# GFNet and FNet halves on one core: C compared with T instead of multiplied, both halves of A in one pass

## The chip, the cores and the metric

The kernel runs on one NeuronCore of one Trainium2 chip. The metric is the device time of one launch in microseconds: 405.52 us before, the median of 3 runs (404.53 to 407.14). A NeuronCore has engines that run side by side and meet at semaphores: TensorE (PE, matmuls into PSUM), VectorE (DVE, elementwise), ScalarE (ACT, copies and functions), GpSimd (POOL) and SyncE (SP, which issues most of the loads). 16 DMA engines carry all transfers.

## What is computed: the reference

Two unrelated results stand side by side in the output, 2048 x 512 each.

```python
# A (GFNet): a filter in the 2-D spectrum of A_x (1, 2048, 512)
X = jnp.fft.rfft2(x, axes=(-2, -1)) * (w_r + 1j * w_i)
a = jnp.fft.irfft2(X, s=(S, D), axes=(-2, -1))

# B (FNet): real part of a 2-D DFT of B_x, with matrices that are inputs
p = jnp.einsum("bsd,ed->bse", x, dft_hid_re)
q = jnp.einsum("bsd,ed->bse", x, dft_hid_im)
b = jnp.einsum("ts,bse->bte", dft_seq_re, p) - jnp.einsum("ts,bse->bte", dft_seq_im, q)
y = jnp.concatenate([a, b], axis=-1)
```

The sequence matrices (2048 x 2048, called C here) arrive as inputs that hold `np.cos(-2.0 * np.pi * ns / S)` and the sine, as float32. The kernel can't take for granted that they do, but it can test it.

## The kernel before

**B.** A sequence transform with the exact cosines and sines needs no large product: the 2048 points are cut into 16 blocks of 128, `b_fft` runs a 16-point transform on DVE over these blocks (`fft16`), `b_slot` does eight small products with tables (`sq`), and `t_rows` multiplies by the hidden matrices (`wd`, L287). What the input C has more than the exact table T is put right by a second way: `prepare` loads 64 pieces of C and of T, builds four quarters of T out of one by copies on ACT (L249, L250), subtracts (L253, DVE), and adds up the absolute difference (L255, ACT) in a column of `stat`. `b_work` multiplies the difference with x (L328, PE, 512 matmuls in f32r), `keep` rounds the sums into SBUF, `rows` multiplies them with `wd` (L305) and DVE adds the two ways' results (L308), which then go out (L311, L313) on POOL's queue. At the end a matmul sums `stat`; if the sum is above `SMALL` = 2^-13, a branch (L770) recomputes B in full in `_b_from_c`.

**A.** The hidden axis is split in two halves of 256 columns (even and odd frequencies), which pass one after the other through: `hidden_fwd` (additions on DVE, L411 to L418, and POOL, L422 and L423, then matmuls L432 and the sums L435, L436 on DVE); `fft16` over 16 blocks; eight slots (`slot`: four additions on POOL, L495 to L498, a matmul L512, the complex product with the weights on DVE, L540 to L542, the folding L557 to L559, matmuls L578, and L584 to L587 on DVE that add and subtract their results); `ifft16`; and `hidden_inv` (matmuls L672, then DVE). The first half's result goes through HBM (`scratch`) and is read back mirrored by a gather (L656), where the second half adds it (L685, L686).

**Order.** The Tile framework orders each engine's instructions by a simulated timeline. The code steers it: `PACE` says how far the other work may fall behind each of the 64 products of B, and `issue_after` holds an instruction behind another. Every engine then runs its own list strictly in turn; a load whose buffer isn't free holds up the loads behind it on SP.

Of the kernel before, what the change touches and what calls it, by code (L numbers as in the profile page):

```python
# [16 lines left out]
P = 128  # L17
# [3 lines left out]
PACE = [3.2] * 9 + [6.3] * 55  # L21
T_ROWS = list(range(13, 29, 2))
SLOTS = [3, 5, 6, 7, 9, 10, 11, 12]
SMALL = 2.0**-13
# [35 lines left out]
def _tables():  # L60
# [22 lines left out]

    b = np.arange(128)
# [15 lines left out]
    tt = np.zeros((2, 4, 4, 128, 2, 2, 256), np.float32)  # L100
    place = (128 * np.arange(8).reshape(4, 1, 2) + b[:, None]).reshape(-1)
    for tb in range(4):
        t = (512 * tb + np.arange(2)[:, None] + 2 * np.arange(256)).reshape(-1)
        th = _ang(np.outer(place, t), S)
        for m, v in enumerate((np.cos(th), -np.sin(th))):
            tt[m, tb] = v.reshape(tt.shape[2:])
    dm = np.zeros((2, 128, 2, 128))
    di = np.zeros((2, 128, 2, 128))
    j = np.arange(128)
    for half in range(2):  # L110
        f = _freqs(half)
        th = _ang(np.outer(j, f), D)
        c, s = np.cos(th), -np.sin(th)
        if half == 0:
            s[:, 0] = np.cos(np.pi * (j % 2))
            dm[half, :, 0] = np.concatenate([c[:, :64], s[:, :64]], 1)
            dm[half, :, 1] = np.concatenate([c[:, 64:], s[:, 64:]], 1)
        else:
            s[0] = -np.sin(_ang(f * 128, D))
            dm[half, :, 0], dm[half, :, 1] = c, s  # L120
        th = _ang(np.outer(f, j), D)
        c, s = 2 * np.cos(th), -2 * np.sin(th)
        if half == 0:
            c[0] = 1.0
            s[0] = np.cos(np.pi * (j % 2))
            di[half, :, 0] = np.concatenate([c[:64], s[:64]])
            di[half, :, 1] = np.concatenate([c[64:], s[64:]])
        else:
            s[:, 0] = -2 * np.sin(_ang(f * 128, D))
            di[half, :, 0], di[half, :, 1] = c, s  # L130
# [9 lines left out]
        "inv": inv.reshape(8, 128, 256).astype(np.float32),  # L140
        "dm": dm.astype(np.float32),
        "di": di.reshape(2, 128, 256).astype(np.float32),
        "sq": sq.astype(np.float32),
        "tt": tt.reshape(2, 4, 4, 128, 2, 512),
        "m0": m0,
        "far": far,
        "mirror": (256 * np.arange(4)[None] + 128 + (-j % 128)[:, None]).astype(np.int32),
# [4 lines left out]
def kernel(  # L152
# [20 lines left out]
    TT = nc.vector.tensor_tensor  # L173
    STT = nc.vector.scalar_tensor_tensor
    ADD, SUB, MUL = ALU.add, ALU.subtract, ALU.mult

# [10 lines left out]
    ps_p = first.enter_context(tc.tile_pool(name="ps_p", bufs=4, space=PSUM))  # L187
    ps_y = first.enter_context(tc.tile_pool(name="ps_y", bufs=1, space=PSUM))
    ps_a = first.enter_context(tc.tile_pool(name="ps_a", bufs=3, space=PSUM))


    xh = bp.tile([P, 16, D], F32R, name="xh")
    wd_sb = bp.tile([P, 2, 4, D], F32, name="wd", bufs=1)
# [6 lines left out]
    zv = ap.tile([P, 16, 256], F32, name="zv")  # L200
# [4 lines left out]
    with tc.tile_pool(name="wp", bufs=1, side="right") as wp:  # L205
        zero = wp.tile([P, 512], mybir.dt.bfloat16, name="zero")
        nc.vector.memset(zero, 0.0)
        warm = ps_a.tile([P, 512], F32, name="pa")
        for _ in range(9):
            nc.tensor.matmul(warm, zero[:, :P], zero, start=True, stop=True)  # L210

    def raw_pair():
        return bp.tile([P, 2, 512], F32, name="raw", bufs=4)

    def row():
        return bp.tile([P, 516], F32, name="yb", bufs=3)
# [7 lines left out]
    items = [(tb, m, q) for tb in (2, 3, 0, 1) for m in range(2) for q in range(8)]  # L224

    def load_x(q, sd):
        rx = load(pt.rearrange("p o m c i -> p (o m c) i")[:, 2 * q : 2 * q + 2], xb[:, q::8, :])
        nc.scalar.copy(xh[:, q::8], rx)
        TT(out=sd[:, q], in0=rx[:, 0], in1=rx[:, 1], op=ADD)
        TT(out=sd[:, 8 + q], in0=rx[:, 0], in1=rx[:, 1], op=SUB)  # L230

    def load_wd():
        for m in range(2):
            load(wd_sb[:, m], wd[m])

    wr = []

    def round_wd():

        wr.append(bp.tile([P, 2, 4, D], F32R, name="wd", bufs=1))  # L240
        for m in range(2):
            nc.gpsimd.dma_start(wr[0][:, m], wd[m])

    def prepare(i):

        tb, m, q = items[i]
        t = bp.tile([P, 2, 2, 256], F32, name="tt", bufs=2)
        load(t[:, 0].rearrange("p o i -> p (o i)"), tabs["tt"][m, tb, q // 2, :, q % 2])
        nc.scalar.copy(t[:, 1, 0], t[:, 0, 0])  # L249
        nc.scalar.mul(t[:, 1, 1], t[:, 0, 1], -1.0)  # L250
        raw = load(raw_pair(), cm[m, tb, q // 2 :: 4, :, q % 2, :].rearrange("r p t -> p r t"))
        e = bp.tile([P, 2, 2, 256], F32R, name="ec", bufs=2)
        TT(out=e, in0=raw.rearrange("p j (i o) -> p j o i", o=2), in1=t, op=SUB)  # L253
        junk = bp.tile([P, 1024], mybir.dt.bfloat16, name="junk", bufs=1)
        nc.scalar.activation(junk, e.rearrange("p j o i -> p (j o i)").bitcast(F32),  # L255
                             mybir.ActivationFunctionType.Abs, accum_out=stat[:, i : i + 1])
        return e

    ps = {}

    def keep(tb, m, acc):


# [53 lines left out]
    def b_work():  # L317
        pending = []
        ready = prepare(0)
        for i, (tb, m, q) in enumerate(items):  # L320
# [3 lines left out]
            if i + 1 < len(items):  # L324
                ready = prepare(i + 1)
# [562 lines left out]
```

## Time and profile before

| | |
|---|---|
| median of 3 runs | 405.52 us (404.53 to 407.14) |
| profiled execution, own time | 409.68 us |
| its span | 407.9 us |
| granted TensorE clock, mean | 0.927 |
| PE busy | 319.5 us, 78% |
| DVE busy | 326.2 us, 80% |
| ACT busy | 179.8 us, 44% |
| POOL busy | 120.3 us, 29% |
| moved by DMA | 90.47 MB, 222 GB/s |

The span is the time between the first and the last thing in the trace; the execution's own time is 1.8 us longer. "Busy" counts a stretch once, though instructions of an engine can overlap. A row of a group reads: line, engine, operation, tiles written and read, shape, count, then the sum of the durations in us and the mean in ns, then how long the engine stood still before these and what ended most of that. A row of the timeline reads: start, duration, engine, line. Rows of the chain have start, duration and what ran.

### The profile page before, as it was taken

Reading aid. Unit: us, or ns where it says so; the run is one execution under the profiler, and the core shown is the slowest. Engines: PE = TensorE matmul, PEld = TensorE weight load, DVE = VectorE, ACT = ScalarE, POOL = GpSimd, SP = SyncE. Lnnn points to the kernel's source line nnn. Section 1 sums busy time; section 2 is a strip of 40 time slices with the busy share of each in tenths; the row PEclk is TensorE's granted clock in tenths of the full one; section 3 lists DMA queues with packets and bytes.
Section 4 is the critical chain, followed back from the end, with each engine's and each line's share of the span. In section 5 each row is a group of like instructions: output and inputs, shape, how many; then the busy total and the mean of one; then the engine's idle time right before and its main releaser. Section 6 shows DMA issues by size and latency. Waiting matters only on the chain.

```text
span 407.9 us, 4458 instructions
## 1 busy us (share of the span) xinstructions
PE 319.5 (78%) x1247; PEld 219.5 (54%) x1247; DVE 326.2 (80%) x601; ACT 179.8 (44%) x398; POOL 120.3 (29%) x158
## 2 busy tenths in 40 slices
PE   3079967999999699999999878998887789800900
PEld 1058745787666366566566557786564557600300
DVE  4999746886983999979987584789949999897662
ACT  4628735668553154423754243665536337100200
POOL 0000005362047739100005153433395850200120
PEclk9999998999999899999999987999999899955755
DMA  7995699876264476523769996697799773300194
GB/s 247 388 405 158 212 305 308 288 286 228 80 191 163 137 241 178 172 90 139 231 217 354 366 408 255 182 300 232 260 299 352 242 203 100 111 9 13 29 338 153
DMA packets 44767, 90.47 MB, mean 222 GB/s; under 512 B 4544, under 2 KB 8896, under 8 KB 44224
## 3 DMA queue, kind: packets, MB, share of 16 engines
q1 hardware_dynamic: 41184, 76.49, 56.9%
q0 software_dynamic: 3552, 13.63, 8.9%
q8 instruction: 12, 0.20, 0.2%
q14 instruction: 19, 0.16, 0.1%
HBM read 79.62 MB, written 10.49 MB: 221 GB/s over the span
## 4 chain that ended last, share of the span: by engine, by line
PE 44%; DVE 25%; DMA 17%; issue 7%; SPq 2%; ACT 1%; POOL 1%; POOLq 0%; DVEq 0%; ACTq 0%
PE acc L328 15%; PE py L287 11%; DMA tt<-tab_tt 7%; DVE ec L253 6%; PE pa L372 5%; DMA raw<-in_cm 3%; DMA xraw<-in_xa 3%; PE pa L578 3%; PE pa L432 2%; PE py L305 2%; SPq L221 2%; PE acc L305 2%; DMA wsp_sb<-in_wsp 2%; DVE m L540 1%; DMA ft<-tab_fwd 1%
## 5 line engine op out<-in xcount | busy, mean ns | idle before, releaser
L328 PE MATMUL acc<-ec,xh 128*128 128x512 f32 x512 | 147.3, 431 | 32.7 <-DVE ec L253 29.4
L328 PEld LDWEIGHTS acc<-ec,xh 128*128 128x128 f32 x512 | 96.5, 194 | 72.4 <-DVE ec L253 38.3
L253 DVE TENSOR_TENSOR ec<-raw,tt 128x1024 fp32r<-128x1024 f32 x64 | 81.1, 1268 | 24.2 <-ACT tt L250 16.6
L255 ACT ACTIVATE junk<-ec 128x1024 bf16<-128x1024 f32 x64 | 67.6, 1056 | 53.6 <-DVE ec L253 53.1
L287 PE MATMUL py<-wd,pt 128*128 128x512 f32 x128 | 59.9, 608 | 0.6 <-DVE yo L572 0.6
L422 POOL TENSOR_TENSOR vf<-uv 128x256 f32<-128x256 f32 x16 | 17.2, 1073 | 138.5 <-DVE uv L415 68.8
L249 ACT COPY tt<-tt 128x256 f32<-128x256 f32 x64 | 26.0, 407 | 69.5 <-DMA tt<-tab_tt 69.5
L287 PEld LDWEIGHTS py<-wd,pt 128*128 128x128 f32 x128 | 24.3, 195 | 26.3 <-issue 24.8
L672 PE MATMUL pa<-zv,di 128*128 128x512 f32 x32 | 17.8, 692 | 22.3 <-DMA di<-tab_di 22.3
L305 PE MATMUL py<-wd,ps 128*128 128x512 f32 x96 | 27.8, 431 | 3.0 <-DVE yb L308 1.8
L250 ACT ACTIVATE tt<-tt 128x256 f32<-128x256 f32 x64 | 26.6, 416 | 0.0
L305 PEld LDWEIGHTS py<-wd,ps 128*128 128x128 f32 x96 | 19.0, 203 | 9.3 <-DMA wd<-in_wd 2.3
L578 PEld LDWEIGHTS pa<-it,yo 128*128 128x128 f32 x128 | 17.8, 199 | 10.4 <-issue 6.6
L578 PE MATMUL pa<-it,yo 128*128 128x128 f32 x128 | 18.7, 287 | 5.5 <-DVE yo L571 3.4
L672 PEld LDWEIGHTS pa<-zv,di 128*128 128x128 f32 x32 | 6.8, 221 | 29.9 <-issue 27.2
L495 POOL TENSOR_TENSOR t<-zv 64x256 f32<-64x256 f32 x14 | 12.4, 885 | 25.7 <-ACT pt L376 21.1
L313 POOL DMA_INDIRECT out_b<-yb,far x8 | 11.4, 1426 | 27.5 <-DVE yb L308 7.1
L376 ACT COPY pt<-pa 128x256 f32<-128x256 f32 x28 | 17.1, 656 | 5.4 <-PE pa L372 5.4
L432 PEld LDWEIGHTS pa<-dm,vf 128*128 128x128 f32 x128 | 17.4, 203 | 2.5 <-issue 1.3
L675 ACT COPY p<-pa 128x512 f32<-128x512 f32 x8 | 4.6, 581 | 31.7 <-PE pa L672 31.7
L540 DVE TENSOR_TENSOR m<-pa,w 128x512 f32<-128x512 f32 x28 | 18.1, 679 | 0.4 <-issue 0.3
L432 PE MATMUL pa<-dm,vf 128*128 128x128 f32 x128 | 17.6, 287 | 0.6 <-DVE um L679 0.6
(200 smaller groups left out, 515.7 us busy)
## 6 DMA issues: line engine op xcount, KB each, us to landing
raw<-in_cm SPq DMA_DIRECT2D x64, 512.0 KB, 7.1
tt<-tab_tt SPq DMA_DIRECT2D x64, 256.0 KB, 3.4
xraw<-in_xa SPq DMA_DIRECT2D x16, 512.0 KB, 5.6
pt<-in_xb SPq DMA_DIRECT2D x8, 512.0 KB, 7.2
w<-in_wa SPq DMA_DIRECT2D x16, 256.0 KB, 4.0
out_a<-xo POOLq DMA_DIRECT2D x4, 1024.0 KB, 5.8
yb<-tab_sq SPq DMA_DIRECT2D x8, 258.0 KB, 7.5
wd<-in_wd SPq DMA_DIRECT2D x2, 1024.0 KB
```

What stands on the lines that cost most here:

```text
L249: nc.scalar.copy(t[:, 1, 0], t[:, 0, 0])
L250: nc.scalar.mul(t[:, 1, 1], t[:, 0, 1], -1.0)
L253: TT(out=e, in0=raw.rearrange("p j (i o) -> p j o i", o=2), in1=t, op=SUB)
L255: nc.scalar.activation(junk, e.rearrange("p j o i -> p (j o i)").bitcast(F32), mybir.ActivationFunctionType.Abs, accum_out=stat[:, i : i + 1])
L287: nc.tensor.matmul(bank, pt[:, o, m, dc, sl], wd_sb[:, m, dc], start=dc == 0, stop=dc == 3)
L305: nc.tensor.matmul(py, ps[tb][:, m, dc, o, h * P : h * P + P], wr[0][:, m, dc], start=m == 0 and dc == 0, stop=m == 1 and dc == 3)
L328: mm = nc.tensor.matmul(acc[dc], xh[:, q + 8 * j, dc * P : dc * P + P], e[:, j].rearrange("p o i -> p (o i)"), start=q == 0 and j == 0, st ...
L372: nc.tensor.matmul(pa[:, :n], z[:, r, dc * P : dc * P + P], sq[:, r, :n], start=r == 0, stop=r == 1)
L432: nc.tensor.matmul(og, vf[:, g, a].rearrange("p h j -> p (h j)"), dm[:, g], start=True, stop=True)
L540: TT(out=mi, in0=x, in1=w[:, i].unsqueeze(2).to_broadcast([P, 2, 2, 128]), op=MUL)
L578: nc.tensor.matmul(pi[:, g_, i].rearrange("p r j -> p (r j)"), yo[:, i, g_].rearrange("p r f -> p (r f)"), it[:, i], start=True, stop=True)
L672: nc.tensor.matmul(pu[g].rearrange("p (a b) -> p a b", a=4), di[:, gs], v[:, g], start=True, stop=True)
```

## The change

1. C is only compared. `prepare`, the products L328, `keep`, `rows`, the f32r copies of x and `wd`, and L308 are gone. `compare` loads 16 pieces of T (a quarter of it, 513 columns) and 64 pieces of C, takes the difference to bf16 on DVE, reading T backwards for two of the four column blocks and with a column of signs for two, and adds up the absolute values on ACT as before. `t_rows` sends B's rows out itself. `SMALL` goes from 2^-13 to 2^-27, so the branch to `_b_from_c` is taken for smaller differences.
2. Both halves of A pass at once, 512 columns wide. x of A is loaded once; `scratch` and the gathers are gone.
3. Sums that DVE did are accumulated by TensorE in PSUM: the two parts in `hidden_fwd` (L435, L436), those after the inverse slot matmuls (L584 to L589), the two groups of the inverse hidden stage and the mirror images there (L678 to L683).
4. Instead of pools that open and close, four regions of 32 KB a partition are used in turn. PSUM holds 3 tiles of two banks and 2 of one.
5. Instead of `PACE`, two lists say at which of 50 steps of A a piece of B (`B_AT`) and how many compares (`C_AT`) are issued. Steps 0 to 7 are `hidden_fwd`, 8 to 12 `fft16`, 13 to 39 the slots, 40 to 45 `ifft16`, 46 to 49 `hidden_inv`. Two compares are left over for the end.

```diff
-PACE = [3.2] * 9 + [6.3] * 55
-SMALL = 2.0**-13
+B_AT = [0, 0, 1, 1, 2, 2, 3, 3] + [4, 5, 6, 7, 7, 7] + [8, 8, 9, 9, 10, 11, 12, 13] + [17, 23, 29, 35, 40, 41, 43, 45]
+C_AT = [0] * 4 + [2] * 4 + [2] * 5 + [0] + [0, 1, 1] * 8 + [0, 0] + [2] * 6 + [4] * 4
+SMALL = 2.0**-27
...
+    def compare():
+        for pr in range(8):
+            ts = []
+            for m in range(2):
+                t = bp.tile([P, 2, 513], F32, name="tt", bufs=3)
+                nc.sync.dma_start(t, tabs["tt"][pr, m])
+                ts.append(t)
+            for tb in range(4):
+                for m, t in enumerate(ts):
+                    v = t[:, :, 512:0:-1] if tb % 2 else t[:, :, :512]
+                    raw = bp.tile([P, 2, 512], F32, name="raw", bufs=3)
+                    nc.sync.dma_start(raw, cm[m, tb, pr])
+                    d = bp.tile([P, 2, 512], mybir.dt.bfloat16, name="ec", bufs=2)
+                    with tc.issue_after(last[0].ins):
+                        if tb in (1, 2):
+                            k = int(tb == 1 and m == 1)
+                            nc.vector.scalar_tensor_tensor(d, v, odd[:, k : k + 1], raw, op0=MUL, op1=SUB)
+                        else:
+                            nc.vector.tensor_tensor(out=d, in0=raw, in1=v, op=ADD if tb and m else SUB)
+                    i = (pr * 4 + tb) * 2 + m
+                    flat = d.rearrange("p j i -> p (j i)")
+                    nc.scalar.activation(flat, flat, mybir.ActivationFunctionType.Abs, accum_out=stat[:, i : i + 1])
+                    yield 1.2
...
     def t_rows(o, b):
...
-                TT(out=pt[:, o, 0, :, sl], in0=us, in1=v, op=SUB)
-                TT(out=pt[:, o, 1, :, sl], in0=us, in1=v, op=ADD)
+                yn, yf = row()[:, :D], row()[:, :D]
+                TT(out=yn.rearrange("p (c f) -> p c f", c=4), in0=us, in1=v, op=SUB)
+                nc.gpsimd.dma_start(out_b[256 * b : 256 * b + 256, :].rearrange("(i o) d -> o i d", o=2)[o], yn)
+                TT(out=yf.rearrange("p (c f) -> p c f", c=4), in0=us, in1=v, op=ADD)
+                nc.gpsimd.indirect_dma_start(
+                    out=out_b, out_offset=bass.IndirectOffsetOnAxis(ap=far_rows[:, 4 * o + b : 4 * o + b + 1], axis=0),
+                    in_=yf, in_offset=None)
...
+    def hidden_fwd(sd):
+        v = region("zv")
+        dm = part(v, 20, 2304)
+        nc.sync.dma_start(dm, tabs["dm"])
...
+        for i in range(8):
+            raw = part(v, 4 * (i % 3), 2, 2, 256)
+            load(raw, xa[1, :, i])
+            u = part(v, 12 + 4 * (i % 2), 2, 2, 256)
+            TT(out=u[:, 0], in0=raw[:, 0], in1=raw[:, 1], op=ADD)
+            w = raw[:, 0]
+            TT(out=w, in0=raw[:, 0], in1=raw[:, 1], op=SUB)
+            STT(u[:, 1, 0], w[:, 1], m0[:, 1:2], w[:, 0], op0=MUL, op1=ADD)
+            STT(u[:, 1, 1], w[:, 0], m0[:, 0:1], w[:, 1], op0=MUL, op1=ADD)
+            ui, vo = (x.rearrange("p e g (a h j) -> p (e g a) h j", a=2, h=2) for x in (u, raw))
+            nc.gpsimd.tensor_tensor(out=vo[:, :, 0], in0=ui[:, :, 0], in1=ui[:, :, 1], op=ADD)
+            nc.gpsimd.tensor_tensor(out=vo[:, :, 1], in0=ui[:, :, 0], in1=ui[:, :, 1], op=SUB)
+            pd = ps_a.tile([P, 2, 2, 256], F32, name="pa")
+            for g in range(2):
+                for a in range(2):
+                    asl = slice(a * 128, a * 128 + 128)
+                    mm(pd[:, 0].rearrange("p s f -> p (s f)"), raw[:, 0, g, asl],
+                                     dm0[:, g, a : a + 2].rearrange("p s f -> p (s f)"),
+                                     start=g == 0 and a == 0, stop=g == 1 and a == 1)
...
+            nc.scalar.copy(sd[:, i::8].rearrange("p s (e f) -> p s e f", e=2), pd.rearrange("p e s f -> p s e f"))
...
+    def slot(e, zv, mid):
...
+        pi = ps_a.tile([P, 2, 2, 256], F32, name="pa")
+        for h in range(2):
+            for g in range(2):
+                for i in range(2):
+                    mm(pi[:, h, g], yo[:, i, h, g], it[:, i], start=i == 0, stop=i == 1)
...
+    def hidden_inv(i, zv):
...
+        for h in (1, 0):
+            for kb in range(2):
+                for g in range(2):
+                    mm(pu[h][:, kb].rearrange("p (a b) -> p a b", a=4), di[:, h, g, kb], v[:, h, g],
+                                     start=g == 0, stop=g == 1)
+        um = part(rb[0], 16 + 4 * (i % 2), 2, 512)
+        nc.scalar.copy(um, pu[1])
+        for h, op in enumerate((ADD, SUB)):
+            xo = part(rb[0], 24 + 4 * h, 2, 512)
+            TT(out=xo, in0=pu[0], in1=um, op=op)
+            nc.gpsimd.dma_start(out_a[256 * h : 256 * h + 256, cols].rearrange("(k p) s -> p k s", p=P), xo)
...
+    while b_at or n < 50:
+        next(a, None)
+        while b_at and b_at[0] <= n:
+            b_at.pop(0)
+            with tc.issue_after(mma[0].ins), tc.issue_after(last[0].ins):
+                next(b, None)
+        for _ in range(C_AT[n]):
+            with tc.issue_after(loads[-1].ins) if n < 8 else ExitStack():
+                next(c)
+        n += 1
```

In all, 62 compares stand at steps (8 in steps 4 to 7, 10 in 8 to 12, 16 among the slots, 12 in 40 to 45, 16 in 46 to 49) and the two left over behind them. `B_AT` puts the loads of B's x at steps 0 to 3, its transform at 4 to 7, its slots at 8 to 13, four `t_rows` among A's slots and four in 40 to 45.

More of the change, by code (lines that the diff above doesn't have):

```diff
@@ L109, in _tables @@
-    j = np.arange(128)
[L110 to L130, printed above, removed]
+    th = _ang(np.outer(np.arange(S), np.arange(513)), S)
@@ L203 @@
     nc.vector.memset(ones, 1.0)
[L205 to L213, printed above, removed]
+    zero = bp.tile([P, 2, 512], mybir.dt.bfloat16, name="ec", bufs=2)[:, 0]
+    nc.vector.memset(zero, 0.0)
+    warm = ps_a.tile([P, 2, 512], F32, name="pa")
+    for _ in range(9):
+        nc.tensor.matmul(warm[:, 0], zero[:, :P], zero, start=True, stop=True)
     def row():
-        return bp.tile([P, 516], F32, name="yb", bufs=3)
+        return bp.tile([P, 516], F32, name="yb", bufs=YB)
     loads = []
@@ L232, in load_wd @@
     def load_wd():
+        rb.append(region("big"))
+        wd_sb.append(part(rb[0], 0, 2, 4, D))
         for m in range(2):
[L234 to L257, printed above, removed]
```

630 lines of the change are left out of this document (247 added, 383 removed).

## The prediction, made before the changed kernel was run

> **What bounds the kernel now.** I read the page's first two parts, then the chain, then the groups by cost.
>
> ```profile
> span 407.9 us, 4458 instructions
> PE 319.5 (78%) x1247; PEld 219.5 (54%) x1247; DVE 326.2 (80%) x601; ACT 179.8 (44%) x398; POOL 120.3 (29%) x158
> PE   3079967999999699999999878998887789800900
> DVE  4999746886983999979987584789949999897662
> PEclk9999998999999899999999987999999899955755
> ```
>
> Two engines share the span: PE and DVE are each at work four fifths of it, and neither has a long empty stretch before the last tenth. So taking work from one alone would stop at the other.
>
> ```profile
> PE 44%; DVE 25%; DMA 17%; issue 7%; SPq 2%; ACT 1%; POOL 1%; POOLq 0%; DVEq 0%; ACTq 0%
> L328 PE MATMUL acc<-ec,xh 128*128 128x512 f32 x512 | 147.3, 431 | 32.7 <-DVE ec L253 29.4
> L253 DVE TENSOR_TENSOR ec<-raw,tt 128x1024 fp32r<-128x1024 f32 x64 | 81.1, 1268 | 24.2 <-ACT tt L250 16.6
> L287 PE MATMUL py<-wd,pt 128*128 128x512 f32 x128 | 59.9, 608 | 0.6 <-DVE yo L572 0.6
> L305 PE MATMUL py<-wd,ps 128*128 128x512 f32 x96 | 27.8, 431 | 3.0 <-DVE yb L308 1.8
> L308 DVE TENSOR_TENSOR yb<-py,pt 128x512 f32<-128x512 f32 x12 | 8.2, 682 | 5.1 <-PE py L305 5.1
> L541 DVE TENSOR_TENSOR y<-m,m 128x256 f32<-128x256 f32 x16 | 8.4, 528 | 0.1
> ```
>
> PE heads the chain, and its costliest group, L328, is the product with C minus T that the change drops. With L305, which multiplies that product by B's second matrix, PE loses over half of its busy time. What is left to set the end is DVE, so I count DVE. Its durations overlap in a row of instructions; the step from start to start is what one costs:
>
> ```profile
> 360.37 0.68 DVE L611 TENSOR_TENSOR E<-T 128x512 f32<-128x512 f32 x1
> 360.97 0.68 DVE L612 TENSOR_TENSOR E<-T 128x512 f32<-128x512 f32 x1
> ...
> 362.17 0.41 DVE L613 SCALAR_TENSOR_TENSOR E<-T 128x256 f32<-128x256 f32 x1
> 362.51 0.41 DVE L614 SCALAR_TENSOR_TENSOR E<-T 128x256 f32<-128x256 f32 x1
> ...
> 387.44 1.22 DVE L685 TENSOR_TENSOR xo<-up,um 128x1024 f32<-128x1024 f32 x1
> 388.57 1.22 DVE L686 TENSOR_TENSOR xo<-up,um 128x1024 f32<-128x1024 f32 x1
> ```
>
> 256 elements a partition cost 0.34 us, 512 cost 0.60, 1024 cost 1.13: 0.07 + 1.04 per 1000 elements. By this line 1536 cost 1.67, 2048 cost 2.20, 128 cost 0.20, and a tiny one 0.07.
>
> **DVE, part by part** (before, then after, us, undisturbed steps):
> - Compare: 64 x 1.13 = 72.6 in both. Half now multiplies by a column of signs first, and 32 of 64 read T backwards. No row shows a backward read; L253 itself reads every second element of C, and its middle duration, 1216 ns in the row further down, is that of L686 in a straight run, so I take nothing. Ends: nothing, or a doubling of 32 of them, +36.
> - A's forward hidden stage: 16 x (0.60 + 4 x 0.34) = 31.4; after, 8 x (2 x 0.60 + 2 x 0.34) = 15.0, since the additions at L435 and L436 become accumulated matmuls.
> - A's 16-point transform: per half 2 x 1.13 + 2 x 0.87 + 0.60 + 26 x 0.34 = 13.4, twice 26.8; after, in one pass as B's, 2 x 2.20 + 2 x 1.67 + 1.13 + 26 x 0.60 = 24.5.
> - Slots: per half and e 2 x 0.60 (L540), 3 x 0.34 (L541, L542, L557), 2 x 0.20, 2 x 0.07, and 0.34 + 2 x 0.20 for L584 to L587: 3.5 x 16 = 56, with e = 0's extras 59. After: 2 x 1.13 + 3 x 0.60 + 2 x 0.34 + 2 x 0.07 = 4.9 x 8 = 39, with extras 42.
> - Inverse 16-point: 2 x (34 x 0.34 + 12 x 0.60) = 37.5; after, 34 x 0.60 + 12 x 1.13 = 34.0.
> - Inverse hidden: 4 x 2 x 0.60 + 4 x (2 x 0.60 + 2 x 1.13) = 18.6; after, 8 x 1.13 = 9.0.
> - L308's additions: 16 x 0.60 = 9.6; after, nothing.
> - Unchanged: loading B 9.6, B's transform 24.5, t_rows 9.6, small ones 1.
>
> Sums: 300 before, 242 after, so 58 less. The page has 326 busy, 26 over my 300. The surplus is seen here (the first and third rows give least, middle and greatest ns):
>
> ```profile
> L253 DVE TENSOR_TENSOR ec<-raw,tt x64: 1202/1216/1875, 21.1 to 341.4; 128x1024 fp32r<-128x1024 f32 x64
> ...
> 134.83 0.96 DVE L542 TENSOR_TENSOR y<-m,m 128x256 f32<-128x256 f32 x1
> ...
> L495 POOL TENSOR_TENSOR t<-zv x14: 719/738/1714, 117.2 to 329.2; 64x256 f32<-64x256 f32 x14
> ```
>
> An operation that takes 0.41 alone took 0.96 beside POOL's, and POOL's own range from 0.72 to 1.71: the two hold each other up. Before, POOL ran 88 such additions (L422, L423, L495 to L498), 88 x 0.72 = 63 us undisturbed. After, it runs 44 of double size; no row has that size, so between 0.72 and 1.44 each, 32 to 63 us. With the surplus in proportion (26 for 63) that is 13 to 26; I take the middle, 20. DVE busy after: 242 + 20 = 262.
>
> **PE.** Steps from the chain:
>
> ```profile
> 107.90 2.59 PE pa L372 x12
> 187.75 3.43 PE py L287 x8
> 191.18 3.75 PE acc L328 x16
> 377.22 3.76 PE pa L672 x4
> ```
>
> A record of 512 columns costs 0.43 in f32 (two records to a matmul), 0.23 in f32r, and 256 columns 0.22. After: B's slots 128 x 0.22 = 28; forward hidden 64 matmuls, 128 x 0.22 = 28; t_rows with the extra row 136 x 0.43 = 58; A's slots 28 x 0.43 + 16 x 0.22 + 128 x 0.22 = 44; inverse hidden 32 matmuls, 64 x 0.43 = 28. Sum 186 against 262 for DVE. The sums that move here double the forward hidden, inverse slot and inverse hidden groups, 3 x 14 = 42 us of PE's free time.
>
> **DMA, ACT, queues.**
>
> ```profile
> HBM read 79.62 MB, written 10.49 MB: 221 GB/s over the span
> raw<-in_cm SPq DMA_DIRECT2D x64, 512.0 KB, 7.1
> 5.74 0.69 DVE L229 TENSOR_TENSOR sdb<-pt 128x512 f32<-128x512 f32 x1 [4.44 <-DMA pt<-in_xb]
> ...
> 15.49 0.69 DVE L229 TENSOR_TENSOR sdb<-pt 128x512 f32<-128x512 f32 x1
> ```
>
> Seven loads of 0.524 MB in 9.75 us are 376 GB/s. After: C 33.6 MB, T 8.4 (16 loads instead of 64), x of A 4.2 (once), x of B 4.2, wd 2.1 (once), sq 2.1, w 4.2, it 2.1, the small tables 2.4, outputs 8.4; scratch is gone. 72 MB are 191 us: no bound as a whole, but one in two places. At the head (steps 0 to 3) dm, four x of A and eight x of B, 7.5 MB, take 20 us plus the first 5, so they end near 25, while DVE has 4 x 1.9 + 9.6 = 17 us to do. At the end (steps 46 to 49 and the rest) 18 compares with T and A's output are 9.4 + 2.1 + 4.2 = 15.7 MB or 42 us, where DVE has 18 x 1.13 + 9.0 = 29 us. Some loads run ahead in three buffers; I add 7 us.
>
> ACT loses L249 and L250, and with them the wait of L253 for L250 (16.6 us above); what is late next for a compare is its load. POOL's queue takes the 16 stores of B's rows, moved from the end into the slots: they stand among the slots' additions, and t_rows on DVE waits for their row buffers, with slot work queued behind it. The same queue loses the four gathers of scratch. In the slots POOL has 28 x 1.44 = 40 us of additions, under DVE's there, so I cost that at nothing; without that cover it is a rival below.
>
> **The sum.** DVE's 262, plus what DVE waits: the head 25 - 17 = 8; the fill of the slots, where slot 1 needs four POOL additions (5.8 us) and a matmul after the last transform step, 7; the end's loads 7; and t_rows in the inverse transform, four groups of 16 records spaced over some 52 us, on a PE that has stood still:
>
> ```profile
> 340.00:360.00 20.00, 14.93 (x80) 12.18 (x78) 18.59 (x52) 5.46 (x14) 2.18 (x4) 0.97 0.25 81
> 360.00:380.00 20.00, 2.78 (x4) 1.25 (x5) 15.05 (x36) 0.59 (x1) 0.00 (x0) 0.50 0.02 7
> 401.20 0.75 POOL L689 DMA_DIRECT2D out_a<-xo  x1 [5.85 <-DVE xo L686]
> ```
>
> In the second row PE was nearly idle and the granted clock was 0.50; L672 then ran its first records in 0.94 (four in 3.76) instead of 0.43. A cold t_rows is 7 us longer; I take 6 us for the part that DVE waits. From the last store's issue at 401.2 to the end are 6.7; with flag and output, 8 at the end. 262 + 8 + 7 + 7 + 6 + 8 = 298, against 407.9. The profiled execution's own time was 409.68, 1.8 over its span; the runs' median 405.52 is 1.0% under it. So 300 x 0.99 = **297 us**.
>
> By the Trainium skill, "TensorE: Matmul & The Clock Gate", section "The HAM clock gate", an idle window of about 3.4 us is enough to halve the clock; the second row agrees in direction, and its rule is weighed as a rival of its own next.
>
> **The rivals.**
> - *The clock falls and stays.* PE is then no longer a filled engine: its 186 us in about 290 leave gaps everywhere. At half clock its slot work and four t_rows are 2 x (44 + 29) = 146 where DVE has about 80, B's slots 56 against 38, the inverse hidden stage 56 against 36: about +66, +18 and +20, 400 us. Against it: in the slots PE would have 73 of 80 us to do, and the row above with PE at 14.93 of 20 was granted 0.97. The skill page named above is the rule behind this rival. Chance 0.05, anywhere from 340 to 400.
> - *The compares starve.* Three buffers and 7.1 us to landing make 2.4 us a compare where they stand densely (30 in steps 40 to 49 and the rest): the last 18 are then 43 us and the twelve before them collide with B's stores. +15 to +30: 320. For it: DMA was already 17% of the chain. Against it: 7.1 was measured beside T's loads, four times as many. Chance 0.17.
> - *POOL and DVE do not overlap at all* where both work. The 63 us of POOL additions (the upper size) then add whole instead of 20: +43, 340. Against it: before, 63 us cost 26. The Trainium skill, "SBUF — State Buffer", section "Who interferes with whom", calls the port the two share an exclusive lock, by which 340 would come out if no POOL addition fell beside DVE work on PSUM; the 0.96 above agrees that one waits for the other. Chance 0.08.
> - *A tight packing*: DVE waits only at head and end, and half of the surplus goes with the half as many POOL instructions: 242 + 13 + 8 + 8 = 271. Chance 0.14.
> - *Slower: the old path is taken.* The threshold on the sum of |C - T| falls from 2^-13 to 2^-27 = 7.45e-9, since nothing corrects B any more. Above it the branch at L770 recomputes B: 1536 + 384 f32r matmuls x 0.23 = 440 us after the 297, so about 740. Working both formulas out in float32 I get 6.54e-9, all of it in about 41,000 entries near zero of at most 1.3e-12. That is 88% of the threshold, and the differences are rounded to bf16 before they are summed, which can move it by a fraction of a per cent. Chance 0.03.
>
> **How the numbers follow.** The forecast, 282 to 312, has 0.53. The range must hold 0.8: from 268, below the tight packing, to 335, which takes in starving compares, the backward reads at double cost (297 + 36 = 333), and half of the port rival. Left out are the cold clock, the old path, half the port rival and the tails, about 0.18. A measurement here tells about 1% from no change, 401.5 to 409.5. Slower: the old path, and a little of the cold clock with mishaps, 0.04; within 1%: the cold clock's upper end, 0.03; faster 0.93.
>
> **What would show it.** DVE busy near 262 and at 85% or more of the span, first in the chain, PE near 190 at full clock. L253's successor at 1.2 to 1.3 each, the backward ones no dearer. POOL's additions at 1.4 or less. In the first 25 us DVE idle on loads; in the last 40 compares waiting for C. A clock row of 5s across the slots, a DVE sum far from 262, compares waiting over 30 us for loads, or instructions of the old path would make it wrong.

## The result and the profile after

The changed kernel takes 340.9 us (median of 4 runs, 340.18 to 342.08) where the kernel before takes 406.33 (4 runs, 404.53 to 408.82): a ratio of 0.8389, 95% interval 0.8336 to 0.8442. It is faster, as forecast, but by 65 us and not by the 110 that the prediction worked out: 340.9 lies above the forecast of 297 and above the upper end of its range, 335. The profiled execution took 340.79 us with a span of 339.0. Three runs of the kernel in experiment 4 (410 to 411 us), one in experiment 9 (344.7) and two of the kernel before (411.8 and 412.4) lie over 1.5% above the fastest run of their kernel, and the ratios and medians below leave them out.

The page of the changed kernel, first its busy times, slices and the engines' shares of the chain, then the groups that matter (the last two with shapes kept apart):

```profile
span 339.0 us, 2463 instructions
...
PE 224.4 (66%) x639; PEld 124.1 (37%) x639; DVE 289.4 (85%) x336; ACT 118.0 (35%) x211; POOL 128.1 (38%) x108
...
PE   4298494429999309208999599699969199980000
...
DVE  1899999999799985899995999999999797558470
...
PEclk9589898959999957856999999999997879995555
...
PE 31%; DVE 27%; DMA 23%; issue 8%; POOL 5%; SPq 2%; ACT 2%; DVEq 0%; ACTq 0%
...
L275 DVE TENSOR_TENSOR ec<-raw,tt 128x1024 bf16<-128x1024 f32 x32 | 44.5, 1404 | 12.4 <-DMA raw<-in_cm 8.9
L273 DVE SCALAR_TENSOR_TENSOR ec<-tt,odd,raw 128x1024 bf16<-128x1024 f32 x32 | 46.1, 1469 | 7.3 <-DMA raw<-in_cm 5.9
...
L368 POOL TENSOR_TENSOR zv<-zv 128x512 f32<-128x512 f32 x8 | 21.8, 2720 | 41.9 <-DVE zv L187 41.9
...
L184 DVE TENSOR_TENSOR big<-pt 128x512 f32<-128x512 f32 x18 | 17.7, 1038 | 0.0
L184 DVE TENSOR_TENSOR sda<-pa,sda 128x1024 f32<-128x1024 f32 x14 | 16.5, 1215 | 0.7 <-issue 0.6
```

In the changed kernel L273 and L275 are the compare (with and without the column of signs), L184 and L187 helpers for DVE's two kinds of operations, L349 the helper for A's matmuls, L288 `t_rows`, L368 and L369 POOL's additions in `hidden_fwd` and L441 to L444 those in the slots.

DVE is now the busiest engine: it is at 85% of the span in 336 instructions, with mostly 9s from the third slice to three quarters of the span. That is what was forecast; that DVE would be first in the chain is not what came, since PE has 31% of it and DVE 27%. And DVE is busy for 289 us, not 262, and it waits for 339 - 289 = 50, not 36. The two surpluses, 27 and 14, are the whole 41 us between the span that was forecast, 298, and the one measured.

Where the 27 are is in the groups. A compare was costed at a step of 1.13, with a duration of 1.2 to 1.3, and has means of 1.40 and 1.47. B's loading additions (`big<-pt`, 512 elements) were costed at 0.60 a step, with durations of 0.69 before, and have a mean of 1.04. But the last row, operations twice as wide that read one operand from PSUM, has 1.22, the duration of an undisturbed one of 1024 elements in the trace of before. The rows by source line, with least, middle and greatest ns, show the compares one by one:

```profile
L273 DVE SCALAR_TENSOR_TENSOR ec<-tt,odd,raw x32: 1274/1281/2303, 60.9 to 326.0; 128x1024 bf16<-128x1024 f32 x32
...
L275 DVE TENSOR_TENSOR ec<-raw,tt x32: 1211/1224/3957, 48.0 to 329.7; 128x1024 bf16<-128x1024 f32 x32
```

Undisturbed, a compare costs what was forecast (1.22, and 1.28 with the signs; half of each group reads T backwards, and with POOL's additions away, in experiment 1, all 32 of L275 lie between 1.22 and 1.23, so that costs nothing). Some cost double or triple. The timelines of DVE and POOL in the first 40 us, with starts and durations, show when:

```profile
11.64 4.62 DVE L184 TENSOR_TENSOR big<-pt 128x512 f32<-128x512 f32 x4
...
33.33 2.49 DVE L184 TENSOR_TENSOR big<-pt 128x512 f32<-128x512 f32 x4
...
11.80 1.64 POOL L368 TENSOR_TENSOR zv<-zv 128x512 f32<-128x512 f32 x1 [11.35 <-DVE zv L187]
13.40 1.70 POOL L369 TENSOR_TENSOR zv<-zv 128x512 f32<-128x512 f32 x1
...
33.64 3.90 POOL L368 TENSOR_TENSOR zv<-zv 128x512 f32<-128x512 f32 x1 [4.95 <-DVE zv L187]
```

At 11.64 four additions of DVE take 4.62 us and the two of POOL beside them little more than their least (1.49 for L368, 1.44 for L369): DVE is held up. At 33.33 the same four take 2.49, as they do in experiment 1 with nothing on POOL, and POOL's L368 beside them takes 3.90: POOL is held up. So POOL's work beside DVE's does not always cost DVE time; which of the two pays differs from meeting to meeting.

Where the 14 are is in the stretches (start and end, length, then busy us and count for PE, PEld, DVE, ACT and POOL, granted clock, DMA share, GB/s):

```profile
120.00:140.00 20.00, 11.46 (x36) 8.58 (x36) 13.17 (x10) 10.78 (x20) 13.34 (x13) 0.71 0.78 279
...
280.00:300.00 20.00, 20.00 (x48) 8.79 (x47) 13.68 (x12) 11.65 (x19) 3.90 (x5) 1.00 0.95 328
300.00:320.00 20.00, 3.62 (x9) 1.33 (x7) 13.11 (x12) 9.06 (x15) 2.86 (x4) 0.64 0.90 328
320.00:339.00 19.00, 0.58 (x2) 0.50 (x2) 8.03 (x9) 8.04 (x14) 0.00 (x0) 0.50 0.44 156
```

In the last 59 us DVE is busy for 34.8 and idle for 24.2, where the prediction had 7 for loads and 8 for the end. DMA is at 90% and more for 40 us of it, and DVE's list of waits over the whole span (total us, times, longest) names C:

```profile
DVE ec L275 <- DMA raw<-in_cm: 8.9, 7, 2.9
DVE ec L273 <- DMA raw<-in_cm: 5.9, 5, 2.8
DVE zv L184 <- DMA zv<-in_xa: 5.0, 2, 4.3
```

### The profile page after: what moved, and what is told of

Same layout as the page of the kernel before. It is cut to its first block, busy times and chain, and to the rows that moved or that the text cites. A ratio compares the mean times of both kernels' runs of the same rounds, so it can differ in the third digit from the quotient of the medians.

```text
span 339.0 us, 2463 instructions
## 1 busy us (share of the span) xinstructions
PE 224.4 (66%) x639; PEld 124.1 (37%) x639; DVE 289.4 (85%) x336; ACT 118.0 (35%) x211; POOL 128.1 (38%) x108
## 2 busy tenths in 40 slices
DMA packets 26260, 71.93 MB, mean 212 GB/s; under 512 B 3200, under 2 KB 8192, under 8 KB 25856
## 4 chain that ended last, share of the span: by engine, by line
PE 31%; DVE 27%; DMA 23%; issue 8%; POOL 5%; SPq 2%; ACT 2%; DVEq 0%; ACTq 0%
PE pa L349 17%; PE pb L288 12%; DMA raw<-in_cm 10%; DVE ec L273 5%; DVE ec L275 4%; DMA yb<-tab_sq 3%; DMA out_b<-yb,far 3%; DMA pt<-in_xb 3%; DVE zv L187 3%; DVE zv L184 3%; DVE big L184 3%; DVE zb L184 2%; DVE pt L184 2%; DVE sda L184 2%; DMA sda<-tab_fwd 2%
## 5 line engine op out<-in xcount | busy, mean ns | idle before, releaser
L278 ACT ACTIVATE ec<-ec 128x1024 bf16<-128x1024 bf16 x64 | 67.6, 1058 | 84.6 <-DVE ec L273 51.4
L349 PE MATMUL pa<-zv 128*128 128x256 f32 (+1 forms) x128 | 49.3, 547 | 31.5 <-POOL zv L369 20.3
L288 PE MATMUL pb<-big,pt 128*128 128x512 f32 x128 | 61.1, 631 | 11.0 <-ACT yb L294 11.0
L275 DVE TENSOR_TENSOR ec<-raw,tt 128x1024 bf16<-128x1024 f32 x32 | 44.5, 1404 | 12.4 <-DMA raw<-in_cm 8.9
L273 DVE SCALAR_TENSOR_TENSOR ec<-tt,odd,raw 128x1024 bf16<-128x1024 f32 x32 | 46.1, 1469 | 7.3 <-DMA raw<-in_cm 5.9
L349 PEld LDWEIGHTS pa<-zv 128*128 128x128 f32 x128 | 26.3, 210 | 55.0 <-POOL zv L369 34.2
L288 PEld LDWEIGHTS pb<-big,pt 128*128 128x128 f32 x128 | 25.5, 202 | 44.0 <-issue 30.0
L368 POOL TENSOR_TENSOR zv<-zv 128x512 f32<-128x512 f32 x8 | 21.8, 2720 | 41.9 <-DVE zv L187 41.9
L184 DVE TENSOR_TENSOR sda<-sda 128x512 f32<-128x512 f32 (+3 forms) x43 | 35.4, 882 | 1.4 <-ACT sda L479 1.1
L349 PE MATMUL pa<-it,sda 128*128 128x256 f32 x128 | 29.8, 388 | 6.6 <-ACT zv L511 3.6
L320 PE MATMUL pb<-yb,zb 128*128 128x256 f32 (+1 forms) x128 | 30.6, 392 | 1.0 <-ACT pt L324 1.0
L349 PEld LDWEIGHTS pa<-it,sda 128*128 128x128 f32 x128 | 24.9, 196 | 14.4 <-issue 6.2
L382 ACT COPY sda<-pa 128x1024 f32<-128x1024 f32 x8 | 8.1, 1010 | 60.5 <-PE pa L349 60.5
L441 POOL TENSOR_TENSOR sda<-zv 64x512 f32<-64x512 f32 x7 | 10.4, 1485 | 46.0 <-DVE zv L187 39.5
L349 PE MATMUL pa<-zv,di 128*128 128x512 f32 x64 | 27.6, 592 | 0.0
L349 PE MATMUL pa<-sda,ft 128*128 128x512 f32 x28 | 15.2, 665 | 15.8 <-POOL sda L448 15.8
L184 DVE TENSOR_TENSOR big<-pt 128x512 f32<-128x512 f32 (+1 forms) x19 | 18.9, 1048 | 0.0
L184 DVE TENSOR_TENSOR sda<-pa,sda 128x1024 f32<-128x1024 f32 (+1 forms) x16 | 17.8, 1149 | 1.2 <-issue 0.6
## 6 DMA issues: line engine op xcount, KB each, us to landing
pt<-in_xb SPq DMA_DIRECT2D x8, 512.0 KB, 10.5
```

What stands on the lines that cost most here:

```text
L184: last[0] = nc.vector.tensor_tensor(**kw)
L273: nc.vector.scalar_tensor_tensor(d, v, odd[:, k : k + 1], raw, op0=MUL, op1=SUB)
L275: nc.vector.tensor_tensor(out=d, in0=raw, in1=v, op=ADD if tb and m else SUB)
L278: nc.scalar.activation(flat, flat, mybir.ActivationFunctionType.Abs, accum_out=stat[:, i : i + 1])
L288: nc.tensor.matmul(bank, pt[:, o, m, dc, sl], wd_sb[0][:, m, dc], start=dc == 0, stop=dc == 3)
L320: nc.tensor.matmul(pa[:, :n], z[:, r, dc * P : dc * P + P], sq[:, r, :n], start=r == 0, stop=r == 1)
```

## The experiments

Ratios are to the kernel before, which took 407.62 us (13 runs), 407.24 (7 runs) and 407.02 (7 runs) on the occasions on which the first four, the next four and the last two ran. Differences between two changed kernels are differences of their medians; "one run" is a single time, without an interval.

**1. POOL's additions away.** If POOL and DVE hold each other up, DVE's surplus goes with the 44 additions.

```diff
-            nc.gpsimd.tensor_tensor(out=vo[:, :, 0], in0=ui[:, :, 0], in1=ui[:, :, 1], op=ADD)
-            nc.gpsimd.tensor_tensor(out=vo[:, :, 1], in0=ui[:, :, 0], in1=ui[:, :, 1], op=SUB)
...
-            PT(out=t[lo, :, 1:3], in0=z[lo, 1], in1=z[lo, 0, :, ::-1], op=ADD)
...
-                mm(flat, ft, t[:, h].rearrange("p i f -> p (i f)"), start=True, stop=True)
+                mm(flat.rearrange("p (r q f) -> p r q f", r=2, q=2), ft, z[:, :, h], start=True, stop=True)
```

> Left out: POOL's 44 additions (16 in the forward hidden stage, 28 in the slots with their four small column fixes); the matmuls read the unfolded data instead, so A's result is another. Theory one, the shared port: DVE's busy time beyond its undisturbed steps (289 - 242 = 47 us) is time in which POOL's additions hold it up, so DVE falls to about 245 to 250 us busy, L275 and L273 to means near 1.22 and 1.28 us, and the time to 290 to 300 us. Theory two, the surplus has another cause (bf16 outputs, the signs, the backward reads, transfers into SBUF): DVE stays above 280 us busy and the time above 330 us.

311.0 us (one run). Its page, busy times and two groups:

```profile
PE 221.8 (72%) x639; PEld 124.1 (40%) x639; DVE 250.1 (81%) x336; ACT 119.3 (39%) x211; POOL 34.9 (11%) x36
...
L275 DVE TENSOR_TENSOR ec<-raw,tt 128x1024 bf16<-128x1024 f32 x32 | 38.8, 1224 | 16.2 <-DMA raw<-in_cm 13.7
L273 DVE SCALAR_TENSOR_TENSOR ec<-tt,odd,raw 128x1024 bf16<-128x1024 f32 x32 | 40.1, 1284 | 9.0 <-DMA raw<-in_cm 7.7
```

DVE has the same 336 instructions and is busy for 39.3 us less; the means fall to the undisturbed values (1224 and 1284, `big<-pt` to 688). So 39 of the 47 us over the undisturbed 242 came from POOL's additions. The other 8 are an error of my sum, most of it in the two rows above: 64 compares, costed at 72.6, take 78.9 undisturbed. (With the additions went 28 column fixes of a few elements on POOL; experiment 2 leaves these in place and finds next to nothing that they cost.) The time fell by 30 and not by 39: DVE's waits grew from 50 to 59 us, and those of compares for C from 14.8 to 21.4. That DVE time isn't the span's is the first thing that the expected 290 to 300 us missed.

**2. The same additions on DVE.** Nothing is left out: the 44 operations move from POOL to DVE.

```diff
-            nc.gpsimd.tensor_tensor(out=vo[:, :, 0], in0=ui[:, :, 0], in1=ui[:, :, 1], op=ADD)
+            TT(out=vo[:, :, 0], in0=ui[:, :, 0], in1=ui[:, :, 1], op=ADD)
...
-            PT(out=t[lo, :, 1:3], in0=z[lo, 1], in1=z[lo, 0, :, ::-1], op=ADD)
+            TT(out=t[lo, :, 1:3], in0=z[lo, 1], in1=z[lo, 0, :, ::-1], op=ADD)
...
```

> The same 44 additions run on DVE instead of POOL, nothing is left out. They cost DVE 44 x 0.60 = 26 us. Theory one (port): the surplus of 47 us goes nearly whole, DVE is at 242 + 26 + 3 = 271 us busy, and the kernel takes 320 to 328 us, less than with POOL's help. Theory two (another cause): DVE 289 + 26 = 315 us busy and about 365 us.

331.96 us (331.31 to 333.05), ratio 0.8148 (0.8126 to 0.817): 9 us faster than the changed kernel, 4 over the upper end of what was expected. The page has DVE at 277.2 us (271 were expected) in 380 instructions: 44 more, and 12 us less. Against the first experiment the additions cost DVE 277.2 - 250.1 = 27.1, or 0.62 each, which is the 0.60 step. Left on POOL they cost DVE 39.3, or 0.89 each, without its doing them.

**3. C loaded once.** If the compares starve for C, taking 63 of its 64 loads away shows how much.

```diff
+                    if not raws:
+                        raws.append(bp.tile([P, 2, 512], F32, name="raw", bufs=3))
+                        nc.sync.dma_start(raws[0], cm[m, tb, pr])
+                    raw = raws[0]
```

> Left out: 63 of the 64 loads of C; every compare reads the first piece, so the test says nothing and its threshold is set out of reach. DVE and ACT work as before. If compares that starve cost the most of what the forecast missed, the time falls by 30 us or more, to 310 or below; if the port does, the waits for C (15 us in the trace) and part of the head's slow loads go and the time falls by 12 to 20 us, to 320 to 328, with DVE still above 280 us busy.

329.7 us (one run), 11 less, just short of the 12 to 20 expected; DVE 286.1 busy. So C's transfers cost about 11 us with everything they collide with, wherever that is. They are not the main cause.

**4. Only the product dropped.** The kernel before, with a part of the first point of the change: the difference goes to bf16 and is added up, and the products with it, `keep`, `rows` and L308 are gone. T is still loaded in 64 pieces and built on ACT; both halves of A, scratch and `PACE` stay, but `PACE` now counts compares, since the products that it counted are gone.

```diff
-            for dc in range(4):
-                for j in range(2):
-                    mm = nc.tensor.matmul(acc[dc], xh[:, q + 8 * j, dc * P : dc * P + P],
-                                          e[:, j].rearrange("p o i -> p (o i)"),
-                                          start=q == 0 and j == 0, stop=q == 7 and j == 1)
+            mm = cmp[-1]
...
-            if pending:
-                rows(*pending.pop(0))
```

> The kernel before with the first part of the change alone: C is compared, not multiplied (no products with the difference, no rounding, no second hidden product; B's rows go out from t_rows). The halves of A, scratch and DVE's sums stay. DVE loses 9.6 us of 326, PE 175 us. If DVE sets the time from here, the kernel is at about 380 to 395 us and the rest of the 66 us gain belongs to the single pass and to the sums on TensorE; if PE was the whole bound, it falls to 350 us or below.

405.48 us (7 runs, 403.66 to 409.08), ratio 0.9951 (0.9916 to 0.9987). Both expectations missed. Its page, its waits of DVE, and one group of matmuls in it (first) and in the kernel before (second):

```profile
PE 191.2 (47%) x607; PEld 111.5 (28%) x607; DVE 310.6 (77%) x585; ACT 153.0 (38%) x354; POOL 110.1 (27%) x156
...
PE   3003791974979689647883000732602385400900
...
DVE  4868996699995665992897997868894799697662
```

```profile
DVE ec L253 <- ACT tt L250: 25.8, 18, 4.3
DVE zv L573 <- ACT bs L571: 10.7, 3, 7.7
```

```profile
L567 PE MATMUL pa<-it,yo 128*128 128x128 f32 x128 | 23.3, 336 | 23.8 <-DVE yo L557 7.0
...
L578 PE MATMUL pa<-it,yo 128*128 128x128 f32 x128 | 18.7, 287 | 5.5 <-DVE yo L571 3.4
```

L328 and L305, 175 us of PE's work, went, and half a per cent of the time with them. DVE lost only 16 us of work, and stands still for 94. The wait for ACT's copies of T grew from 16.6 us (before) to 25.8, and PE has gaps all along. With the gaps its granted clock fell from 0.927 to 0.733, and what it still does got slower, as the last two rows show: PE's busy time fell by only 128 us (319.5 to 191.2). PE's 44% of the chain of before was a share, not a price. How much a PE at the old clock would have given back, and how much only less work on DVE and another order could give, this run doesn't tell apart. Dropping the product alone is worth next to nothing, so the 65 us need the other parts of the change: one pass of A, the sums on PE, T loaded and not built, and the order. Of these only one kind of sum is taken apart below.

**5. Only the forward hidden additions on DVE** (the first pair of lines of experiment 2; the 28 of the slots stay on POOL).

> Only the 16 additions of the forward hidden stage move from POOL to DVE (16 x 0.60 = 9.6 us); the slots' 28 stay on POOL. Port theory: the additions of B's x, B's transform and the first compares lose their surplus, some 20 to 25 us of the 47, so DVE is at about 275 to 280 us busy and the time at 325 to 332 us, no worse than with all 44 moved (332), since the slots' share pays 17 us to save about 20. If the forward hidden stage isn't where it hurts, DVE is at 295 us or more and the time is not below 340.

330.67 us (329.21 to 332.94), ratio 0.8103 (0.8035 to 0.8172), with DVE 279.3 busy. It can't be told from moving all 44, so as far as this pair tells, the cost in time sits with the 16 that PE waits for before its forward products (in the changed kernel, 20.3 us of PE's waits are for L369).

**6. One kind of sum back on DVE.** The two parts in `hidden_fwd` are again added on DVE, with a copy by ACT, and PE multiplies half the columns.

```diff
-                    mm(pd[:, 0].rearrange("p s f -> p (s f)"), raw[:, 0, g, asl],
-                                     dm0[:, g, a : a + 2].rearrange("p s f -> p (s f)"),
-                                     start=g == 0 and a == 0, stop=g == 1 and a == 1)
+                    mm(pd[:, a, 0], raw[:, 0, g, asl], dm0[:, g, 0], start=g == 0, stop=g == 1)
...
-            nc.scalar.copy(sd[:, i::8].rearrange("p s (e f) -> p s e f", e=2), pd.rearrange("p e s f -> p s e f"))
+            nc.scalar.copy(tt_, pf[:, 1])
+            TT(out=sd[:, i], in0=pf[:, 0], in1=tt_, op=ADD)
+            TT(out=sd[:, 8 + i], in0=pf[:, 0], in1=tt_, op=SUB)
```

> One of the four kinds of sums undone: in the forward hidden stage TensorE no longer adds the two parts; ACT copies one out of PSUM and DVE adds and subtracts, 16 operations of 512 from PSUM, 16 x 0.60 = 9.6 us; PE does half the columns there. If DVE sets the time, the kernel is 6 to 10 us slower than the changed one (347 to 351 us). If the chain through PE set it (the matmuls of this stage are 41 us at full clock), it is no slower or faster (330 to 341 us).

357.48 us (356.44 to 359.01), ratio 0.8768 (0.8705 to 0.8832): 16.6 us slower than the changed kernel, more than the 6 to 10 expected if DVE sets the time, though DVE's busy time is 7 us lower (282.3). The list of DVE's waits has a new first row:

```profile
DVE sda L184 <- ACT zv L381: 20.5, 4, 6.0
```

So this kind of sum is worth 16.6 us on PE. It is no work saved on DVE but a wait saved (DVE stands still for 73 us instead of 50): the addition stands in DVE's list behind PE and ACT, and all of DVE's later work stands behind the addition.

**7 and 8. Compares earlier, with the additions on DVE; then the loads of `wd` through POOL's queue too.** Nine compares move from the end to steps 4 to 12.

```diff
-C_AT = [0] * 4 + [2] * 4 + [2] * 5 + [0] + [0, 1, 1] * 8 + [0, 0] + [2] * 6 + [4] * 4
+C_AT = [0] * 4 + [3] * 4 + [3] * 5 + [0] + [0, 1, 1] * 8 + [0, 0] + [2] * 6 + [2] * 4
...
-            load(wd_sb[0][:, m], wd[m])
+            nc.gpsimd.dma_start(wd_sb[0][:, m], wd[m])
```

> All 44 additions on DVE, and nine compares moved from the four steps of the inverse hidden stage and the end to steps 4 to 12 (3 a step there instead of 2, 2 a step at the end instead of 4). If the end starves for C, the waits for C there (18 us) fall to 6 to 10 us, and the time goes from 332 to 318 to 325 us. If the loads are as late earlier, because the loads' queue stands still behind buffers in steps 4 to 12, the time stays within 3 us of 332.

> As the one before, and the two loads of the hidden matrices go through POOL's queue, so that the loads of C behind them on SP no longer wait until B's transform has left the region they go to (SP waits there 23 us, and DMA stands nearly still from 66 to 83 us). If this queue is what keeps early compares from their data, another 4 to 8 us go, to 312 to 320 us; if not, no difference beyond 2 us.

321.48 us (319.48 to 322.76), ratio 0.7882 (0.7817 to 0.7946), and 320.91 (319.88 to 321.86), ratio 0.7863 (0.7808 to 0.7918). The early compares are worth 10.5 us against experiment 2, as expected; the queue of the `wd` loads is worth nothing that can be measured. DVE's waits for C in experiment 2 (first two rows) and in 7 (last two):

```profile
DVE ec L273 <- DMA raw<-in_cm: 9.5, 6, 3.1
DVE ec L275 <- DMA raw<-in_cm: 8.9, 6, 3.7
```

```profile
DVE ec L275 <- DMA raw<-in_cm: 5.4, 3, 3.6
...
DVE ec L273 <- DMA raw<-in_cm: 3.4, 2, 2.7
```

DVE's busy time is the same (277.2 and 276.1), so the gain is in waits: those for C, 18.4 us, became 8.8. These two kernels beat both the kernel before and the changed one.

**9. Compares earlier alone.** The same list with POOL's additions left where the change has them: is the end's cost independent of POOL's?

> The changed kernel with nothing moved but compares: five of the 16 compares of the last four steps go to the start's steps with four more of the same kind taken from the two left over and the end (the same list as in the run with the additions on DVE); POOL's additions stay on POOL. If the end's compares starve for C, as the run with C loaded once (11 us) and the run with additions on DVE and early compares (10 us) say, independently of POOL: 330 to 333 us, waits of compares for C down from about 15 to 5 to 9 us. If the 10 us came from the two edits together (compares put beside POOL's hidden additions now stretch each other): 336 to 341.

336.63 us (3 runs, 335.67 to 337.61), ratio 0.8266 (0.8216 to 0.8316): 4.3 us, not 10, and inside what was expected if the two belong together. A stretch of its timeline shows what took the rest:

```profile
60.05 4.49 DVE L273 SCALAR_TENSOR_TENSOR ec<-tt,odd,raw 128x1024 bf16<-128x1024 f32 x2
61.22 2.24 POOL L369 TENSOR_TENSOR zv<-zv 128x512 f32<-128x512 f32 x1
...
63.51 8.29 PE L349 MATMUL pa<-zv 128*128 128x512 f32 x16 [8.95 <-POOL zv L369]
...
71.84 1.01 ACT L382 COPY sda<-pa 128x1024 f32<-128x1024 f32 x1 [16.23 <-PE pa L349]
72.75 1.06 ACT L278 ACTIVATE ec<-ec 128x1024 bf16<-128x1024 bf16 x1
...
73.93 1.28 DVE L273 SCALAR_TENSOR_TENSOR ec<-tt,odd,raw 128x1024 bf16<-128x1024 f32 x1 [8.19 <-ACT ec L278]
...
76.24 8.58 POOL L368 TENSOR_TENSOR zv<-zv 128x512 f32<-128x512 f32 x1 [12.78 <-DVE zv L187]
```

Read from the bottom up: a compare on DVE stands still for 8.19 us, because both buffers of differences wait for ACT to add them up; ACT's list has a copy (L382) ahead of that, which waits for PE; PE waited for POOL's L369 and ran cold afterwards: 8.29 us for 8 records of 512 columns and 8 of 256, with a granted clock of 0.50 from 62 to 68 us; the same 16 take 5.43 at 28.75 in the changed kernel, with 1.00 granted. One late addition on POOL stops DVE through three other engines' lists. And the last row is a POOL addition of 8.58 us, where the least of its line is 1.49.

**10. Forward hidden additions on DVE, early compares, `wd` by POOL's queue.**

> The 16 additions of the forward hidden stage on DVE, the 28 of the slots left on POOL, early compares, the tables of the hidden matrices loaded through POOL's queue. If the slots' additions on POOL cost nothing beyond their stretch of DVE's work (the run with only the hidden ones moved came out 1 us under the run with all moved): 319 to 322 us, equal to the 321 with all 44 on DVE. If they cost time in the slots once the end no longer waits: 323 to 327.

324.67 us (322.67 to 326.77), ratio 0.8001 (0.7935 to 0.8067). Against experiment 8 the slots' 28 additions cost 3.8 us on POOL. In experiment 5, with the end still waiting for C, they could not be told from nothing.

## Why the prediction was right and wrong

**Right: the direction, the new bound, the undisturbed steps.** DVE became the busiest engine, and its steps came out as the lines of the trace of before gave them: compares at 1.22 to 1.28, backward reads free, 250 us in all without POOL's additions, against the 242 summed. The moved bytes (71.93 MB against 72) fit, and so does the head (DVE idle for 9.5 us in the first 40, 8.3 of it for loads, against 8). The old path was not taken and the clock did not stay low (23 of the 40 slices in the row of the clock are 9s). That taking work from PE alone stops at the other engine fits experiment 4, as far as the slower clock there lets it tell.

**Right by luck: the fill of the slots.** The row from 120 to 140 has DVE idle for 6.8 us, against 7. But the sum had four POOL additions and a matmul for it, and the waits there are others: 2.6 for loads of C, 3.0 for ACT's copies in the first slot and 1.2 for ACT's adding up.

**Wrong: "With the surplus in proportion (26 for 63) that is 13 to 26; I take the middle, 20".** It measured 289 - 242 = 47, of which experiment 1 puts 39 down to POOL's additions and 8 to the sum. The two traces, counted operation by operation, show what the proportion missed. Before, 39 DVE operations beside POOL's 88 additions took longer than the undisturbed ones of their shape, by 0.54 us in the middle and 20 us in all; so 20 of the 26, and not all, were POOL's. After, 37 operations beside 44 additions of double size took longer, by 1.06 us in the middle and 40 us in all, the 39 of experiment 1. Half as many additions held up about as many DVE operations, each for twice as long: 40 us, where the proportion took half the instructions or the same undisturbed time and so 13 to 26.

I did not ask how often an addition would meet a DVE operation that it can hold up. DVE standing still explains little of it: 70 of the 84 us of POOL's additions fell beside busy DVE before, and 81 of 83 after. More comes from what DVE did there: 21 us fell beside operations that read PSUM before and 5.5 after (the change moved sums of that kind to TensorE), and 49 and 73 us beside operations with both inputs in SBUF. (That this is why the meetings became more frequent is argued from the two traces; that the additions cost 39 is shown.) POOL's side was mis-sized with it: 44 additions at 1.44 or less would be 63 us at most, and the groups L368, L369 and L441 to L444 add up to 84 (L368 21.8 of it).

The rival *POOL and DVE do not overlap at all* gave 340 with a chance of 0.08 and came out nearest. Its mechanism is largely right, but that its time is within 1 us of the 340.9 is luck: it adds the whole 63 us where the runs have 39, and 14 of the 41 us that were missing are waits. By the Trainium skill, "SBUF — State Buffer", section "Who interferes with whom", a DVE instruction with two inputs in SBUF contends with a GpSimd instruction that reads SBUF, one with at most one SBUF input, outside the DVE modes that use two ports, doesn't, and the lock is exclusive. The trace agrees: of the 18 `big<-pt`, two inputs in SBUF, 13 ran beside a POOL addition and took 1.18 on average, the other five 0.68; of the 14 `sda<-pa,sda`, one input in PSUM, five did and took 1.22, like those that didn't.

**Wrong: the end, "I add 7 us" for loads and 8 for the rest.** DVE stood still for 24 us in the last 59, so the terms were short by 9; the mechanism (18 compares with T and A's output need longer to move than DVE needs to work) was the one named. The rival *compares starve*, 15 to 30 us, describes it too, at about 11 (experiment 3) and 10.5 (experiment 7 against 2). The other 5 of the 14 are single short waits, the longest about 2 us, that the sum did not have. The 6 for a cold `t_rows` in the inverse transform were not paid there: DVE waited 4.1 us for L288, 3.8 of it between 181 and 185 among the slots, where the granted clock was 1.00.

**Wrong without effect: PE.** 224 busy, against 186. I counted the 64 records of the forward hidden stage's first product as 256 columns wide; they are 512 wide, 64 x (0.43 - 0.22) = 13 us more. The groups, with shapes kept apart, show them:

```profile
L349 PE MATMUL pa<-zv 128*128 128x512 f32 x64 | 36.0, 715 | 31.5 <-POOL zv L369 20.3 <-ACT ec L278 11.2
```

These 64 records are busy for 36.0 us, 0.56 each, where 0.43 is the step at full clock; their mean duration is 715 ns, against 592 for records of the same shape in `pa<-zv,di`, which ran at 0.43 each (durations overlap). PE ran cold after gaps, 0.74 granted from 60 to 80 us, but POOL's additions are not the reason: with them away, in experiment 1, the same group has 36.1 and 717. That PE heads the chain with 31% has its own reason: from 160 to 240 us PE is busy for 73 of 80 us at a granted clock of 1.00, nearly as much as DVE's 75, and most of the chain there is PE's.

**What stays open.** How the 65 us divide between one pass of A, the remaining kinds of sums, T by loads and the written order was not taken apart: each needs the others' buffers. Nor is it shown what decides, when an addition of POOL and an operation of DVE meet, which of the two is held up.

## What to carry to other kernels

When a change makes an engine the bound, cost anew what its neighbours do to it: an addition on POOL cost DVE about 0.2 us before (20 us for 88) and 0.89 after, with double the size, more than the 0.62 of doing it there. An engine's share of the chain is no price: 175 us of TensorE's work came out for half a per cent of the time. DVE's work and the order stayed much the same, and the rest of TensorE's work ran at a lower clock; the run doesn't tell the two apart. And where engines run their lists in turn, look for the instruction that stands far down a chain of three engines (experiments 6 and 9): it holds up everything behind it, whatever its own length.

## What the hardware showed that was not expected

- POOL's operations stretch far more than DVE's: an addition of 128 x 512 took from 1.44 to 6.31 us in the changed kernel and up to 8.58 in experiment 9, in both cases beside a dense run of DVE work. DVE's compares went from 1.22 to at most 3.96.
- Issuing an indirect store on POOL stretches too, from 1.0 to 8.12 us, beside dense DVE work between 259 and 267. The timeline of the changed kernel shows what that set off:

```profile
259.37 8.12 POOL L300 DMA_INDIRECT out_b<-yb,far  x1 [4.94 <-DVE zb L187]
...
269.38 0.59 ACT L294 COPY yb<-pb 128x512 f32<-128x512 f32 x1 [8.12 <-DMA out_b<-yb,far]
...
270.01 6.14 PE L288 MATMUL pb<-big,pt 128*128 128x512 f32 x8 [7.15 <-ACT yb L294]
```

  ACT waited 8.12 us for the row buffer that this store frees and PE 7.15 for ACT, and then ran cold (6.14 for 8 records, with 0.50 granted from 270 to 274, against 3.60 at 181.5 with 1.00). That DVE's work caused the long issue is argued from the timing; no run took it away alone.
- A column of signs as a third operand costs 0.06 us on 1024 elements, and reading backwards nothing.
